# A linear-attention mix on one core: where the output weights are split, a second q buffer, and two tiles' products on VectorE

## The chip, the core and the metric

The kernel runs on one core of a Trainium2 chip. Five engines work side by side, each through its own instructions in program order: TensorE (PE, matrix products into PSUM), VectorE (DVE), ScalarE (ACT), GpSimd (POOL) and SyncE (SP), which here issues every DMA. An instruction that waits holds up all that stand behind it on its engine; engines wait for each other, and for DMAs, by semaphores. The metric is the device time of one execution in microseconds, the median of several runs.

## What is computed

Two branches A and B share the input x (2048 tokens of 448 features) and have their own weights. Each is a linear attention with 16 heads of 28 features and a learned feature map made of two softmaxes; a sigmoid gate mixes them.

```python
qkv = (x @ wqkv).reshape(B, S, 3, H, Dh)            # H = 16, Dh = 28
pq = einsum("bhsd,hdf->bhsf", q, w_phi)              # the same for k
phi_q = concatenate([softmax(pq), softmax(-pq)], -1) # the same for k
kv = einsum("bhsf,bhsd->bhfd", phi_k, v)
z  = einsum("bhsf->bhf", phi_k)
num = einsum("bhqf,bhfd->bhqd", phi_q, kv)
den = einsum("bhqf,bhf->bhq", phi_q, z)[..., None] + 1e-6
branch = (num / den).reshape(B, S, D) @ wo
...
g = sigmoid((x * gate_w).sum(-1, keepdims=True))
out = g * branch_A + (1 - g) * branch_B
```

## The kernel before

The tokens go through in 16 tiles of 128. To keep precision, a matrix is cut into a high part (rounded to the format that TensorE takes) and a low part, the remainder; a product is high x high + low x high + high x low. `split_w` (L99) makes the two parts of a weight: ACT copies the high part, another engine subtracts.

Phase 1 is the loop at L253, one step a tile. PE projects keys (`proj` with `wkh`, `wkl`) and values (`wvh`, `wvl`), 44 matmuls a step, and adds the previous tile to the 56-column sums of keys and values in PSUM (`kv_acc`, L177). DVE makes maxima, minima and shifted values (`shift`), ACT the exponentials, DVE their sums and POOL the quotients (`k_soft`). In steps 2 to 5 the query weights are folded out of `wtb`, a buffer of 4096 columns that holds the raw key and query weights and later, from step 14, the transposed query exponentials of two tiles. In the last three steps the query side of tiles 0 and 1 is begun: `q_front` (L192) subtracts the maximum into `uq`, and SP moves it to DRAM in four pieces and back into `tq` in another order, so that heads stand on partitions. Raw output weights lie in DRAM as `wos`, written there in step 0 in an order of their own.

Between the phases (L303 to L324) come `q_front` of tiles 2 and 3, which write the one buffer `uq` in turn; then the output weights, seven chunks of 128 rows, each loaded from `wos` into one half of `ob` (tile `bd`), split by ACT and POOL into `woh` and `wol` (tiles `wkh` and `wkl`, whose key weights are no longer needed); then the copy of the sums into `kvs` on ACT (L314), their transposition and finish into `kvt` on DVE and POOL; then `gates` of the last three tiles: an exponential on ACT, two DVE instructions, a DMA to DRAM (`gd`), four DMAs back into `gate`, and one POOL instruction (L250).

Phase 2 is the loop at L404. In step i, PE makes the numerators and denominators of tile i (`num`, 256 small matmuls), the query projection of tile i + 4 and the output of tile i - 2 (`out_mm`, 21 matmuls). DVE turns the numerators (`n_turn`) and makes reciprocals; POOL multiplies and adds (`n_rec`, `n_mix`: small products, then L364, the product over 1792 elements, and L367, the sum of the two softmax halves); DVE turns the result back (`o_turn`), ACT makes its high part, DVE and POOL (L386) the low one. Tiles `wvh` and `wvl`, once the value weights, hold the numerators of even and odd tiles in their first 2048 columns and part of the turned result in the next 384.

The order on each engine is that of the code; nothing reorders it.

Of the kernel before, what the change touches and what calls it, by code (L numbers as in the profile page):

```python
# [30 lines left out]
def hedgehog_mix(ctx: ExitStack, tc: tile.TileContext, xd, wv, wkt, wqt, wphi, wo, cmask, cpmask, out):  # L31
# [67 lines left out]
    def split_w(wr, wh, wl, eng):  # L99
        nc.scalar.activation(wh, wr, AF.Copy)  # L100
        eng.tensor_tensor(wl, wr, wh.bitcast(F32), OP.subtract)
# [90 lines left out]
    def q_front(k, ps):  # L192
        seq[k] = len(seq) % 2
        mx = work.tile([P, 2, H], F32, name="qmx")
        p4 = hb(ps[:, :, :D])
        nc.vector.tensor_reduce(mx, p4, AX.X, OP.max)
        for b in range(2):
            nc.vector.tensor_tensor(uq[:, :, b], p4[:, b].rearrange("p (r g) f -> p r g f", r=4),  # L198
                                    mx[:, b].rearrange("p (r g) -> p r g", r=4)[:, :, :, None].to_broadcast([P, 4, 4, DH]),
                                    OP.subtract)  # L200
# [3 lines left out]
        nc.sync.dma_start(tq[seq[k]].rearrange("p c b g f -> p (c b g f)"), m.rearrange("r t c x -> (r t) (c x)"))
# [21 lines left out]
    def q_turn(k):  # L226
        nc.vector.transpose(e_slot(k), eq.rearrange("p s a c f -> p (s a c f)"))  # L227

# [8 lines left out]
    def two_tile():  # L239
        return two.tile([P, 2, 512], F32, name="two")  # L240
# [12 lines left out]
    for t in range(NT):  # L253
# [92 lines left out]

    def n_rec(i):
        rs = work.tile([P, 8, 2, 4], F32, name="crs")
        dd = work.tile([P, 8, 2, 4], F32, name="cdd")
        den = work.tile([P, 4, 2, 4], F32, name="cden")  # L350
        sms[i] = rs, dd, den
        cv = ctrs[i % 2].rearrange("p r b s c m -> p (r b) s c m")
        nc.vector.reciprocal(rs, cv[:, :, :, :, DH + 1])
        nc.gpsimd.tensor_tensor(dd, cv[:, :, :, :, DH], rs, OP.mult)
        nc.gpsimd.tensor_tensor(den.rearrange("p r b c -> p (r b) c"), dd[:, :, 0], dd[:, :, 1], OP.add)

    def n_mix(i):
        rs, dd, den = sms.pop(i)
        nc.vector.reciprocal(den, den)
        nc.gpsimd.tensor_tensor(den, den, gate[:, None, :, :, i].to_broadcast([P, 4, 2, 4]), OP.mult)  # L360
        nc.gpsimd.tensor_tensor(dd, rs, den.rearrange("p r b c -> p (r b) c")[:, :, None, :].to_broadcast([P, 8, 2, 4]),
                                OP.mult)
        c3 = ctrs[i % 2].rearrange("p r b s c m -> p (r b s c) m")[:, :, :DH]
        nc.gpsimd.tensor_tensor(c3, c3, dd.rearrange("p a s c -> p (a s c)")[:, :, None].to_broadcast([P, 64, DH]), OP.mult)  # L364
        o = os_[i] = ph.tile([P, 4, 8, DH], F32, name=f"vs{i % 2}", bufs=1)
        c4 = ctrs[i % 2].rearrange("p r b s c m -> p (r b) s c m")
        nc.gpsimd.tensor_tensor(o.rearrange("p c a f -> p a c f"), c4[:, :, 0, :, :DH], c4[:, :, 1, :, :DH], OP.add)  # L367

# [108 lines left out]
```

## Time and profile before

| what | us |
|---|---|
| median of three runs | 416.49 |
| lowest and highest run | 414.44, 417.14 |
| the profiled execution | 414.41 |
| its span, first to last instruction | 412.6 |

| engine | busy us in the span | share |
|---|---|---|
| PE matmul | 360.6 | 87% |
| DVE | 283.3 | 69% |
| POOL | 233.7 | 57% |
| ACT | 122.9 | 30% |

The page cuts the span into 40 slices of 10.3 us and writes the busy share of each in tenths (9 is 90% or more). PEclk is the clock granted to TensorE, in tenths of full speed.

```profile
PE   7999999999999999999720068999999999997875
```

The digits 2, 0, 0, 6 stand for 206 to 247 us, the passage between the phases. DVE's and POOL's rows have the same hole, and the row of the clock falls to 5 there. In the rows further down, a line of the chain of waits reads: start, duration, engine, tile written, line; a line of the timeline adds the shapes, the count and, in brackets, how long the engine had idled and what released it.

### The profile page before, as it was taken

The page shows a single profiled execution, that of the slowest core. Times are in us where ns is not written, and L with a number is a line of the kernel's source. Part 1 is how long each engine was busy: PE and PEld are TensorE (multiplying, and loading weights), DVE is VectorE, ACT ScalarE, POOL GpSimd, SP SyncE. Part 2 cuts the span into 40 slices and gives each one's busy share as a digit, 9 for nine tenths or more (in the row PEclk, how much of TensorE's full clock was granted, in tenths as well). Part 3 has the DMA queues.
Part 4 walks back from the last instruction along what each step waited for, and adds up shares of the span by engine and source line. Part 5 has one row for each costly group of instructions (what it writes and reads, how often), then busy time and mean ns, then how long its engine had stood idle before and what let it go on. Part 6 is the DMA issues. An engine that isn't in the chain of part 4 may idle for free.

```text
span 412.6 us, 10388 instructions
## 1 busy us (share of the span) xinstructions
PE 360.6 (87%) x4608; PEld 318.8 (77%) x4608; DVE 283.3 (69%) x309; ACT 122.9 (30%) x174; POOL 233.7 (57%) x194
## 2 busy tenths in 40 slices
PE   7999999999999999999720068999999999997875
PEld 7799999999999998998610057888888888875654
DVE  2676667676666666688400079999999999988821
ACT  2634353422222222124011302333323233333112
POOL 0285646164333333143113349999988888889991
PEclk9999999999999999999975558999999999999989
DMA  7937403000000000312432113254433333330101
GB/s 185 286 124 215 175 27 103 2 0 2 2 2 2 2 2 4 89 24 68 119 104 71 41 27 102 82 132 116 113 112 102 100 102 108 113 115 24 48 22 44
DMA packets 24913, 32.09 MB, mean 78 GB/s; under 512 B 3476, under 2 KB 19844, under 8 KB 24836
## 3 DMA queue, kind: packets, MB, share of 16 engines
q1 hardware_dynamic: 24868, 31.43, 26.0%
q8 instruction: 36, 0.59, 0.6%
q14 instruction: 9, 0.07, 0.1%
HBM read 20.40 MB, written 12.62 MB: 80 GB/s over the span
## 4 chain that ended last, share of the span: by engine, by line
PE 65%; DMA 10%; POOL 10%; DVE 7%; SPq 3%; issue 2%; ACT 2%; DVEq 0%; POOLq 0%; ACTq 0%
PE two L134 32%; PE out L393 12%; PE q L134 11%; PE num L339 5%; DMA bd<-wos 5%; PE one L184 3%; DMA qd<-uq 2%; POOL xrb L215 2%; PE two L119 2%; DMA xrb<-in_xt 2%; POOL wvh L364 2%; POOL wvl L364 2%; POOL vs L367 2%; DMA tq<-qd 1%; DVE uq L198 1%
## 5 line engine op out<-in xcount | busy, mean ns | idle before, releaser
L164 POOL TENSOR_TENSOR e<-e,rs 128x896 f32<-128x896 f32 x32 | 53.8, 1703 | 76.7 <-DVE rs L161 70.1
L153 ACT ACTIVATE e<-e 128x896 f32<-128x896 f32 x32 | 30.2, 954 | 112.4 <-DVE e L150 112.3
L393 PE MATMUL out<-wkh,e 128*128 128x448 f32 x224 | 53.7, 376 | 9.6 <-POOL e L386 6.2
L339 PE MATMUL num<-wtb,kvt 32*32 32x128 f32 x2048 | 32.3, 295 | 30.5 <-POOL kvt L318 28.1
L339 PEld LDWEIGHTS num<-wtb,kvt 32*32 32x32 f32 x2048 | 25.6, 107 | 37.6 <-POOL kvt L318 28.4
L393 PEld LDWEIGHTS out<-wkh,e 128*128 128x128 f32 x224 | 41.9, 191 | 16.3 <-POOL e L386 7.7
L134 PE MATMUL two<-wkh,xg 128*128 128x448 f32 x224 | 52.1, 370 | 0.7 <-POOL xg L86 0.4
L134 PE MATMUL two<-wvh,xg 128*128 128x450 f32 (+1 forms) x224 | 50.9, 366 | 0.0
L146 DVE TENSOR_REDUCE mx<-two 128x32 f32<-128x896 f32 x16 | 17.5, 1092 | 42.1 <-PE two L134 42.1
L134 PE MATMUL q<-wqh,xg 128*128 128x448 f32 x168 | 40.9, 384 | 5.6 <-DVE uq L198 5.6
L134 PEld LDWEIGHTS two<-wkh,xg 128*128 128x128 f32 x224 | 40.9, 188 | 5.1 <-POOL xg L86 0.7
L134 PEld LDWEIGHTS two<-wvh,xg 128*128 128x128 f32 x224 | 42.1, 188 | 3.3
L215 POOL TENSOR_TENSOR xrb<-qmn,tq 128x896 f32<-128x896 f32 x16 | 28.1, 1759 | 23.0 <-DVE qmn L214 19.2
L134 PEld LDWEIGHTS q<-wqh,xg 128*128 128x128 f32 x168 | 31.7, 194 | 10.9 <-issue 6.6
L227 DVE STREAM_TRANSPOSE wtb<-xrb 128x2048 f32<-128x2048 f32 x16 | 36.9, 2304 | 3.4 <-ACT xrb L219 3.4
L160 DVE TENSOR_REDUCE sm<-e 128x32 f32<-128x896 f32 x32 | 33.3, 1082 | 1.1
L134 PE MATMUL two<-wvl,xg 128*128 128x450 f32 (+1 forms) x128 | 31.1, 365 | 0.0
L134 PE MATMUL two<-wkl,xg 128*128 128x448 f32 x128 | 30.8, 362 | 0.0
L376 ACT ACTIVATE e<-turn 128x512 fp32r<-128x512 f32 x16 | 9.6, 599 | 69.0 <-DVE turn L373 69.0
L393 PE MATMUL out<-wkl,e 128*128 128x448 f32 x112 | 26.2, 373 | 0.0
L364 POOL TENSOR_TENSOR wvh<-wvh,cdd 128x1792 f32<-128x1792 f32 x8 | 25.8, 3224 | 0.6
L364 POOL TENSOR_TENSOR wvl<-wvl,cdd 128x1792 f32<-128x1792 f32 x8 | 25.8, 3222 | 0.6
(81 smaller groups left out, 617.4 us busy)
## 6 DMA issues: line engine op xcount, KB each, us to landing
qd<-uq SPq DMA_DIRECT2D x64, 112.0 KB, 2.2
tq<-qd SPq DMA_DIRECT2D x16, 448.0 KB, 3.0
out<-bd SPq DMA_DIRECT2D x16, 224.0 KB, 3.4
xrb<-in_xt SPq DMA_DIRECT2D x3, 1024.0 KB
wvr<-in_wv SPq DMA_DIRECT2D x4, 449.0 KB
wtb<-in_wkt SPq DMA_DIRECT2D x8, 224.0 KB, 6.9
wtb<-in_wqt SPq DMA_DIRECT2D x2, 896.0 KB
wos<-in_wo SPq DMA_DIRECT2D x2, 784.0 KB
```

The lines of the kernel that those rows point to most:

```text
L134: nc.tensor.matmul(ps[:, b, :n], x[:, xc, o:o + P], w[:, wc, lo:lo + n], start=i == 0, stop=i == len(terms) - 1)
L146: nc.vector.tensor_reduce(mx[:, 0], p4, AX.X, OP.max)
L153: nc.scalar.activation(e[:, s], e[:, s], AF.Exp)
L160: nc.vector.tensor_reduce(sm[:, s], e[:, s].rearrange("p (h f) -> p h f", f=DH), AX.X, OP.add)
L164: nc.gpsimd.tensor_tensor(e3, e3, rs[:, s, :, None].to_broadcast([P, HA, DH]), OP.mult)
L184: nc.tensor.matmul(kvp[32 * r:32 * r + DH + 1, b, g], v[:, b, h // 2, h % 2], phi[:, :, hs:hs + DH], start=(t == 0 and b == 0 and g == 0), ...
L215: nc.gpsimd.tensor_tensor(eq[:, 1, :, :, :DH], mn.rearrange("p c a -> p a c")[:, :, :, None].to_broadcast([P, 8, 4, DH]), tview(k), OP.sub ...
L227: nc.vector.transpose(e_slot(k), eq.rearrange("p s a c f -> p (s a c f)"))
L339: nc.tensor.matmul(ps[32 * g:32 * g + 32, r, 2 * b + s], kvt[32 * r:32 * r + 32, b, s, g], eTs[i][32 * r:32 * r + 32, s, b, g], start=True ...
L364: nc.gpsimd.tensor_tensor(c3, c3, dd.rearrange("p a s c -> p (a s c)")[:, :, None].to_broadcast([P, 64, DH]), OP.mult)
L376: nc.scalar.activation(hl[:, 0, :MID], ps, AF.Copy)
L393: nc.tensor.matmul(ps[:, :D], a, w, start=n == 0, stop=n == len(terms) - 1)
```

## The change

Four edits.

- A function `split_wo(c)` does one chunk of the output weights: load from `wos` into `wtb`, split on ACT and POOL within `wtb`, and store both parts to DRAM (`wod`). It runs in steps 6 to 12 of phase 1, one chunk a step, the chunks alternating between two places in `wtb`. Between the phases two loads bring the whole of `woh` and `wol` back, 12,544 bytes a partition each.
- `q_front` takes its buffer from a list `uqs`. The list gets a second entry after tile 2: columns 2560 to 3455 of tile `wvh`, so that tiles 3, 5, 7 and so on use that one.
- The tiles `wvh` and `wvl` are taken over for numerators before `q_front(3)` and no longer after the sums.
- In `n_rec` and `n_mix` the last two tiles (14 and 15) use VectorE for the six products and sums that GpSimd does for the others.

```diff
+    wod = [dram.tile([P, 7, D], F32, name=f"wod{i}") for i in range(2)]
...
     def q_front(k, ps):
         seq[k] = len(seq) % 2
+        u = uqs[k % len(uqs)]
...
-            nc.vector.tensor_tensor(uq[:, :, b], p4[:, b].rearrange("p (r g) f -> p r g f", r=4),
+            nc.vector.tensor_tensor(u[:, :, b], p4[:, b].rearrange("p (r g) f -> p r g f", r=4),
...
+    def split_wo(c):
+        n = 3 * D * (c % 2)
+        st = [wtb[:, n + D * i:n + D * i + D] for i in range(3)]
+        nc.sync.dma_start(st[0], wos[:, HP * c:HP * (c + 1), :])
+        split_w(st[0], st[1].bitcast(F32R), st[2].bitcast(F32R), nc.gpsimd)
+        for i in range(2):
+            nc.sync.dma_start(wod[i][:, c], st[1 + i])
...
-            uq = qp.tile([P, 4, 2, 4, DH], F32, name="uq")
+            uqs = [qp.tile([P, 4, 2, 4, DH], F32, name="uq")]
...
         if t > 0:
             kv_acc(t - 1, phi.pop(t - 1))
+        if 6 <= t < 13:
+            split_wo(t - 6)
         if t == NT - 4:
             gates(0, t + 1)
...
-    for k in (2, 3):
-        q_front(k, proj(k, wqh, wql, (D, D), two_tile()))
+    q_front(2, proj(2, wqh, wql, (D, D), two_tile()))
+    cb = [wp_.tile([P, 3592], F32, name=n) for n in ("wvh", "wvl")]
...
+    uqs.append(cb[0][:, 2560:2560 + 2 * D].rearrange("p (r b g f) -> p r b g f", r=4, b=2, g=4))
+    q_front(3, proj(3, wqh, wql, (D, D), two_tile()))
     woh = wp_.tile([P, 7, D], F32R, name="wkh")
     wol = wp_.tile([P, 7, D], F32R, name="wkl")
+    for w, d in ((woh, wod[0]), (wol, wod[1])):
+        nc.sync.dma_start(w.bitcast(F32), d)
     ob = wp_.tile([P, 2, D], F32, name="bd")
     obs = [ob[:, i] for i in range(2)]
-    for c in range(7):
-        nc.sync.dma_start(obs[c % 2], wos[:, HP * c:HP * (c + 1), :])
-        split_w(obs[c % 2], woh[:, c], wol[:, c], nc.gpsimd)
     kv_acc(NT - 1, phi.pop(NT - 1))
...
     def n_rec(i):
+        eng = nc.vector if i >= NT - 2 else nc.gpsimd
...
-        nc.gpsimd.tensor_tensor(dd, cv[:, :, :, :, DH], rs, OP.mult)
+        eng.tensor_tensor(dd, cv[:, :, :, :, DH], rs, OP.mult)
...
-        nc.gpsimd.tensor_tensor(c3, c3, dd.rearrange("p a s c -> p (a s c)")[:, :, None].to_broadcast([P, 64, DH]), OP.mult)
+        eng.tensor_tensor(c3, c3, dd.rearrange("p a s c -> p (a s c)")[:, :, None].to_broadcast([P, 64, DH]), OP.mult)
```

What stands on the engines at the three places that the prediction speaks of. Names with a number are buffers of the pool of that name; a line number is that of the kernel that the list is from. First SP, the queue of DMAs, from the copy-back of query tile 2 to the first stores of phase 2. Before:

```order
L204 DMA tq_293<-qd_81 128x896
L203 DMA qd_82<-uq 32x4x224 x4
L204 DMA tq_294<-qd_82 128x896
L310 DMA bd<-wos 128x1x448 x7
L247 DMA gd<-glog 128x3
L249 DMA gate<-gd 32x4x3 x4
L203 DMA qd_81<-uq 32x4x224 x4
```

The same place after:

```order
L206 DMA tq_295<-qd_83 128x896
L205 DMA qd_84<-wvh 32x4x224 x4
L206 DMA tq_296<-qd_84 128x896
L325 DMA wkh<-wod_80 128x3136
L325 DMA wkl<-wod_81 128x3136
L258 DMA gd<-glog 128x3
L260 DMA gate<-gd 32x4x3 x4
L205 DMA qd_83<-uq 32x4x224 x4
```

Seven chunk loads have become two long ones at the same place, ahead of the last gates' DMAs, and tile 3 is stored from `wvh`.

POOL, from the last step of phase 1 to the first products of phase 2 (`e` are the key exponentials, `wkl` the low output weights, `xrb` the query exponentials). Before:

```order
L164 TENSOR_TENSOR e<-e,rs 128x896 x2
L101 TENSOR_TENSOR wkl<-bd,wkh 128x448 x7
L317 MEMSET kvt 128x16
L318 TENSOR_SCALAR kvt<-kvt 128x2x4
L250 TENSOR_SCALAR gate<-gate 128x4x3
L354 TENSOR_TENSOR cdd<-wvh,crs 128x64
```

After:

```order
L165 TENSOR_TENSOR e<-e,rs 128x896 x2
L333 MEMSET kvt 128x16
L334 TENSOR_SCALAR kvt<-kvt 128x2x4
L261 TENSOR_SCALAR gate<-gate 128x4x3
L368 TENSOR_TENSOR cdd<-wvh,crs 128x64
```

The seven subtractions have left this place (each now stands behind the two `e` products of a step from 6 to 12); the gates' instruction is still ahead of the first products.

DVE in step 15 of phase 2, from the turning of the numerators to the low part of tile 14 (`turn` and `wvh` are the turned result, `cden` and `cdd` the small factors, `vs` the mixed result). Before:

```order
L345 STREAM_TRANSPOSE wvl<-num 128x2048
L353 RECIPROCAL crs<-wvl 128x64
L373 STREAM_TRANSPOSE turn<-vs_4046 128x512
L374 STREAM_TRANSPOSE wvh<-vs_4046 128x384
L359 RECIPROCAL cden<-cden 128x32
L382 TENSOR_TENSOR e<-turn,e 128x512
```

After:

```order
L358 STREAM_TRANSPOSE wvl<-num 128x2048
L367 RECIPROCAL crs<-wvl 128x64
L368 TENSOR_TENSOR cdd<-wvl,crs 128x64
L369 TENSOR_TENSOR cden<-cdd 128x32
L388 STREAM_TRANSPOSE turn<-vs_4064 128x512
L389 STREAM_TRANSPOSE wvh<-vs_4064 128x384
L374 RECIPROCAL cden<-cden 128x32
L375 TENSOR_TENSOR cden<-cden,gate 128x32
L376 TENSOR_TENSOR cdd<-crs,cden 128x64
L379 TENSOR_TENSOR wvl<-wvl,cdd 128x64x28
L382 TENSOR_TENSOR vs_4174<-wvl 128x8x4x28
L397 TENSOR_TENSOR e<-turn,e 128x512
```

Six instructions have come over from POOL, in front of the low part (L382 before, L397 after), which the last third of the output product reads.

More of the change, by code (lines that the diff above doesn't have):

```diff
@@ L202, in q_front @@
         for c in range(4):
-            nc.sync.dma_start(m[:, :, c].rearrange("r t x -> t r x"), uq[32 * c:32 * c + 32].rearrange("p r b g f -> p r (b g f)"))
+            nc.sync.dma_start(m[:, :, c].rearrange("r t x -> t r x"), u[32 * c:32 * c + 32].rearrange("p r b g f -> p r (b g f)"))
         nc.sync.dma_start(tq[seq[k]].rearrange("p c b g f -> p (c b g f)"), m.rearrange("r t c x -> (r t) (c x)"))
@@ L300, in hedgehog_mix @@
             q_front(n, proj(n, wqh, wql, (D, D), two_tile()))
-    for k in (2, 3):
-        q_front(k, proj(k, wqh, wql, (D, D), two_tile()))
+    q_front(2, proj(2, wqh, wql, (D, D), two_tile()))
+    cb = [wp_.tile([P, 3592], F32, name=n) for n in ("wvh", "wvl")]
+    ctrs = [c[:, :2048].rearrange("p (r b s c m) -> p r b s c m", r=4, b=2, s=2, m=HP) for c in cb]
+    oTs = [c[:, 2048:2048 + (7 - MID) * P].rearrange("p (k t) -> p k t", t=P) for c in cb]
+    uqs.append(cb[0][:, 2560:2560 + 2 * D].rearrange("p (r b g f) -> p r b g f", r=4, b=2, g=4))
+    q_front(3, proj(3, wqh, wql, (D, D), two_tile()))
     woh = wp_.tile([P, 7, D], F32R, name="wkh")
     wol = wp_.tile([P, 7, D], F32R, name="wkl")
+    for w, d in ((woh, wod[0]), (wol, wod[1])):
+        nc.sync.dma_start(w.bitcast(F32), d)
     ob = wp_.tile([P, 2, D], F32, name="bd")
     obs = [ob[:, i] for i in range(2)]
-    for c in range(7):
-        nc.sync.dma_start(obs[c % 2], wos[:, HP * c:HP * (c + 1), :])
-        split_w(obs[c % 2], woh[:, c], wol[:, c], nc.gpsimd)
     kv_acc(NT - 1, phi.pop(NT - 1))
@@ L318, in hedgehog_mix @@
     nc.gpsimd.tensor_scalar(kvt[:, :, 0, :, DH], kvt[:, :, 0, :, DH], 1e-6, None, op0=OP.add)
-    cb = [wp_.tile([P, 3592], F32, name=n) for n in ("wvh", "wvl")]
-    ctrs = [c[:, :2048].rearrange("p (r b s c m) -> p r b s c m", r=4, b=2, s=2, m=HP) for c in cb]
-    oTs = [c[:, 2048:2048 + (7 - MID) * P].rearrange("p (k t) -> p k t", t=P) for c in cb]
     gates(NT - 3, NT)
@@ L353, in n_rec @@
         nc.vector.reciprocal(rs, cv[:, :, :, :, DH + 1])
-        nc.gpsimd.tensor_tensor(dd, cv[:, :, :, :, DH], rs, OP.mult)
-        nc.gpsimd.tensor_tensor(den.rearrange("p r b c -> p (r b) c"), dd[:, :, 0], dd[:, :, 1], OP.add)
+        eng.tensor_tensor(dd, cv[:, :, :, :, DH], rs, OP.mult)
+        eng.tensor_tensor(den.rearrange("p r b c -> p (r b) c"), dd[:, :, 0], dd[:, :, 1], OP.add)
     def n_mix(i):
         rs, dd, den = sms.pop(i)
+        eng = nc.vector if i >= NT - 2 else nc.gpsimd
         nc.vector.reciprocal(den, den)
-        nc.gpsimd.tensor_tensor(den, den, gate[:, None, :, :, i].to_broadcast([P, 4, 2, 4]), OP.mult)
-        nc.gpsimd.tensor_tensor(dd, rs, den.rearrange("p r b c -> p (r b) c")[:, :, None, :].to_broadcast([P, 8, 2, 4]),
+        eng.tensor_tensor(den, den, gate[:, None, :, :, i].to_broadcast([P, 4, 2, 4]), OP.mult)
+        eng.tensor_tensor(dd, rs, den.rearrange("p r b c -> p (r b) c")[:, :, None, :].to_broadcast([P, 8, 2, 4]),
                                 OP.mult)
         c3 = ctrs[i % 2].rearrange("p r b s c m -> p (r b s c) m")[:, :, :DH]
-        nc.gpsimd.tensor_tensor(c3, c3, dd.rearrange("p a s c -> p (a s c)")[:, :, None].to_broadcast([P, 64, DH]), OP.mult)
+        eng.tensor_tensor(c3, c3, dd.rearrange("p a s c -> p (a s c)")[:, :, None].to_broadcast([P, 64, DH]), OP.mult)
         o = os_[i] = ph.tile([P, 4, 8, DH], F32, name=f"vs{i % 2}", bufs=1)
         c4 = ctrs[i % 2].rearrange("p r b s c m -> p (r b) s c m")
-        nc.gpsimd.tensor_tensor(o.rearrange("p c a f -> p a c f"), c4[:, :, 0, :, :DH], c4[:, :, 1, :, :DH], OP.add)
+        eng.tensor_tensor(o.rearrange("p c a f -> p a c f"), c4[:, :, 0, :, :DH], c4[:, :, 1, :, :DH], OP.add)
     def o_turn(i):
```

## The prediction, made before the changed kernel was run

> **What bounds the kernel now.** I read the stage table first (busy time of each engine in stretches of the span), then the chain of work that ended last, then the timeline where the chain leaves TensorE. Columns of the stage table: stretch, its length, busy us of PE, PEld, DVE, ACT and POOL with instruction counts, granted TensorE clock, DMA share, GB/s.
>
> ```profile
> 0.00:206.00 206.00, 200.17 (x1971) 181.49 (x1972) 136.20 (x146) 67.14 (x88) 81.62 (x58) 1.00 0.24 71
> 206.00:236.50 30.50, 2.44 (x14) 1.89 (x12) 0.94 (x3) 5.46 (x11) 8.27 (x9) 0.61 0.23 75
> 236.50:255.60 19.10, 14.19 (x406) 11.48 (x406) 15.66 (x18) 3.86 (x5) 12.25 (x14) 0.65 0.21 52
> 255.60:364.40 108.80, 108.73 (x1711) 95.30 (x1711) 102.79 (x112) 35.24 (x51) 95.58 (x82) 1.00 0.39 110
> 364.40:412.60 48.20, 35.07 (x510) 28.68 (x510) 27.73 (x31) 11.19 (x20) 36.03 (x33) 0.96 0.12 44
> ```
>
> PE is full in phase 1 (to 206) and again from 255.6 to 364.4; both stretches are worth nothing to a change that leaves PE's work alone. The 30.5 us from 206.0 are nearly idle on every engine, the next 19.1 are a start-up in which PE is not the bound, and the last 48 are a tail in which POOL is busier than PE. The change works on these three. The chain through the hole:
>
> ```profile
> 207.48 0.34 SPq L204
> ...
> 207.87 5.77 DMA bd<-wos
> ...
> 213.67 0.58 ACT wkh L100
> ...
> 214.32 1.14 POOL wkl L101
> ...
> 229.02 5.08 DMA bd<-wos
> ```
>
> Four such rounds, the last from 229.02, follow one another (load, high part on ACT, low part on POOL, next load into the freed buffer). ACT, in program order, cannot copy `kvs` before the last of them, so `num(0)` starts at 236.5.
>
> **Phase 1, where the splitting goes.** Seven steps (t = 6 to 12) each get one load of 224 KB, one ACT copy, one POOL subtraction, two stores. Rows of step 12 and 13:
>
> ```profile
> 151.87 0.16 ACT L170 ACTIVATE glog<-two 128x1 f32<-128x1 f32 x1
> 153.07 3.36 POOL L164 TENSOR_TENSOR e<-e,rs 128x896 f32<-128x896 f32 x2 [6.65 <-DVE glog L245]
> 159.29 1.89 ACT L153 ACTIVATE e<-e 128x896 f32<-128x896 f32 x2 [7.01 <-DVE e L150]
> ```
>
> ACT is free for 7.0 us before each step's exponentials and POOL for about 6.6 of 10; the added 0.58 on ACT and 1.14 on POOL fit. SP takes its DMAs in order, so load c+1 is issued once POOL has done chunk c and the low store has gone out: 153.07 + 3.36 + 1.14 + about 0.6 = 158.2 in these terms. With a landing of 5.0 to 5.8 (chain rows above) it is there at 163 to 164; ACT reaches its copy at about 162.0 and waits 1 to 2 us of its 7. The step stays PE's: cost 0. If a load took over 7.3 us the loop load + 0.58 + 1.14 + 1.0 would pass the 10.0 us step (that is a rival below). In step 12 the DMAs of the first 13 gates queue on SP behind the last low store, so POOL's gate instruction, which waits for them, comes some 5 us later. That falls into POOL's idle 6.6 and pushes the next L164 by 1 us at most; its reader, the accumulation a step later, has 10: cost 0. The last store has some 50 us before it is read.
>
> **The doubled q buffer.** It removes a wait on DVE (in brackets):
>
> ```profile
> 199.67 0.99 PE L184 MATMUL one<-e,vs 128*29 128x56 f32 x64
> 202.29 0.34 SPq L204 DMA_DIRECT2D tq<-qd  x1
> 202.37 1.16 DVE L198 TENSOR_TENSOR uq<-two,qmx 128x448 f32<-128x448 f32 x2 [1.50 <-DMA qd<-uq]
> 203.67 1.67 PE L134 MATMUL q<-wqh,xg 128*128 128x448 f32 x7 [3.01 <-DVE uq L198]
> ```
>
> L198 ends at about 202.0 instead of 203.53, and PE's first q tile, which waits for it, starts at 202.1. But SP stays in order: the copy-back of tile 2 still waits on tile 2's store (202.29), the stores of tile 3 go out behind that, from 202.7, so what follows on SP is only about 1 us earlier: copy-back of tile 3 at 206.4 (was 207.48). In phase 2 the buffer's earlier reader is a step old and nothing there waited for it: 0.
>
> **The hole and what takes its place.** ACT now copies `kvs` after the accumulation (199.67 + 0.99), DVE turns it after L198 at 202.0, POOL finishes `kvt` at about 203.3, and `num(0)` runs behind the first q tile at 202.1 + 4.75 = 206.9, 29.6 us earlier. It does not follow that the kernel gains 29.6, since phase 2 also needs the last gates. In program order POOL stands at L250 (gates 13 to 15) ahead of every product of tile 0, and SP now has two loads of 1.6 MB ahead of the gates' DMAs. The start-up before:
>
> ```profile
> 236.22 0.35 SPq L247 DMA_DIRECT2D gd<-glog  x1
> 237.72 2.25 SPq L249 DMA_DIRECT2D gate<-gd  x4
> 241.33 0.20 POOL L250 TENSOR_SCALAR gate<-gate 128x12 f32<-128x12 f32 x1 [4.89 <-DMA gate<-gd]
> 242.34 0.35 POOL L354 TENSOR_TENSOR cdd<-wvh,crs 128x64 f32<-128x64 f32 x1 [0.81 <-DVE crs L353]
> 242.76 0.25 POOL L355 TENSOR_TENSOR cden<-cdd 128x32 f32<-128x32 f32 x1
> 243.28 1.75 POOL L215 TENSOR_TENSOR xrb<-qmn,tq 128x896 f32<-128x896 f32 x1 [0.26 <-DVE qmn L214]
> 245.06 0.95 ACT L219 ACTIVATE xrb<-xrb 128x896 f32<-128x896 f32 x1 [8.94 <-POOL xrb L215]
> 245.64 2.98 PE L134 MATMUL q<-wqh,xg 128*128 128x448 f32 x7 [1.10 <-DVE uq L198]
> 246.04 2.31 DVE L227 STREAM_TRANSPOSE wtb<-xrb 128x2048 f32<-128x2048 f32 x1 [0.46 <-ACT xrb L219]
> 255.67 4.75 PE q L134 x22
> ```
>
> Behind POOL stand DVE's reciprocal (L359) and, behind that on DVE, the q work that frees PE's next tile: all wait on G, the time at which L250 runs. When do the gates land? Speed and order of the queue:
>
> ```profile
> 6.40 7.08 DMA xrb<-in_xt
> 7.88 2.69 SPq L97 DMA_DIRECT2D wvr<-in_wv  x4
> 2.00:13.00 11.00, 10.20 (x72) 9.27 (x71) 3.75 (x7) 1.83 (x2) 0.00 (x0) 1.00 1.01 237
> 46.00:48.00 2.00, 2.00 (x14) 1.88 (x11) 1.09 (x1) 0.08 (x1) 2.00 (x2) 1.00 1.04 401
> 213.00:214.00 1.00, 0.00 (x0) 0.00 (x0) 0.00 (x0) 0.33 (x1) 0.00 (x0) 0.50 0.26 100
> ```
>
> The first x piece (256 KB, behind 1.9 MB of key weights) landed at 13.48, when about 237 GB/s x 11 us = 2.6 MB had moved, though 1.8 MB of value weights were queued behind it from 7.88: an early DMA is mostly served first. So I take the gates to come behind both loads. A load with all engines at work moves 401 GB/s (46 to 48) and the old chunk loads 100 on a quarter of them (213 to 214). The new loads have 128 rows of 12.5 KB, contiguous on both sides, so I take 401, and 200 as the far end. Copy-back issued 206.4, its data 207.5 to 209.0 (an estimate: 1.1 from issue to data, 448 KB at 300 to 400); 2 x 128 x 3136 x 4 B = 3.21 MB / 401 = 8.0 us, to 217.0. Of the 1.5 us that `gd` needs alone (236.22 to 237.72) about 1.1 lie ahead of its data, so it lands at about 217.9. From the first gate DMA to POOL 3.6 (237.72 to 241.33): G = 221.5.
>
> Where page and row differ: the Trainium skill, "DMA: Bandwidth & Descriptors", Bandwidth, holds HBM traffic of one core to about 358 GB/s. By it the loads take 9.0 us and every time below would be 1.0 later; the row of 401 in this trace is over that, and I stay with the row.
>
> From G on: 0.20 + 0.35 + 0.25 and the gaps, then L215 1.75, ACT 0.95, so the transposition L227 starts at G + 3.8 (it was G + 4.7, DVE's L353 came last there). From it to PE's first back-to-back q tile 255.67 - 246.04 = 9.6 us of DVE work, unchanged. PE comes to its second q tile after some 12 us of idling; before, its first 7 matmuls took 2.98 (245.64) where 22 take 4.75 at full clock (255.67), that is 1.5 for 7. A tile half of which runs so slowly ends about 0.7 after DVE asks for it at the latest; I take 0.4. So PE is full from 221.5 + 3.8 + 9.6 + 0.4 = 235.3 instead of 255.67: **20.4 us gained**. The output weights are needed only 4.7 us later still, at 240: hidden. From there the 108.8 us of full PE are unchanged.
>
> **The tail.** Tiles 14 and 15 leave POOL for DVE.
>
> ```profile
> 385.64 0.95 POOL e L386
> ...
> 393.83 0.95 POOL e L386
> ...
> 404.57 4.54 PE out L393 x21
> 382.78:389.38 6.60, 4.88 (x143) 3.76 (x141) 4.92 (x7) 1.55 (x3) 5.82 (x8) 1.00 0.06 23
> L364 POOL TENSOR_TENSOR wvl<-wvl,cdd 128x1792 f32<-128x1792 f32 x8 | 25.8, 3222 | 0.6
> L367 POOL TENSOR_TENSOR vs<-wvl 128x896 f32<-128x896 f32 x8 | 16.9, 2110 | 0.6
> L101 DVE TENSOR_TENSOR wvl<-wvr,wvh 128x898 fp32r<-128x898 f32 x3 | 3.1, 1088 | 0.0
> L101 POOL TENSOR_TENSOR wvl<-wvr,wvh 128x898 fp32r<-128x898 f32 x1 | 2.5, 2513 | 3.4 <-ACT wvh L100 3.4
> ```
>
> DVE does 898 elements from SBUF in 1.09, so the product takes about 2.1 (was 3.22) and the sum 1.1 (was 2.11); the four small ones I put at 0.15 each (0.25 to 0.35 on POOL). But DVE already had 4.9 us of work in a tail step (382.78 to 389.38, seven instructions from one turning of numerators to the next). With 3.8 more and the gaps it is 8.9 a step, against POOL's 8.2 before (393.83 - 385.64). So POOL's bound is exchanged for DVE's, and only the overlap of tiles 13 and 14 is gained. From tile 13's sum at 385.64 DVE needs some 5.8 for the turn of tile 13 and the products of tile 14: 391.4; step 15 takes 8.9: 400.3; the last turn and ACT's two copies behind it 2: 402.3. The last 21 matmuls start at 402.6, or at 403.8 if tile 14's run slow at a lower clock (0.96 in the tail as a whole), instead of 404.57: 0.8 to 2.0, I take **1.4**. Bounds: 0 if DVE's products cost as on POOL less the hand-overs, 3 if the small ones are free.
>
> The Trainium skill, "GPSIMD Engine Reference", Specifications, says POOL shares its SBUF interface with DVE and is held up by DVE instructions with two SBUF inputs, which these products are. This trace bears it out weakly (POOL's own 898-wide L101 ran beside DVE's; twice the 448-wide 1.14 of 214.32 would be 2.28, it took 2.51); here it would delay only L386, which ends before DVE's own L382, so the sum stays.
>
> **Sum.** Profiled execution before 414.41 (span 412.6): 414.4 - 20.4 - 1.4 = 392.6. That execution lies 2.1 below the shown median of 416.49 and at the lowest of the three (414.44); I put the median at 394.
>
> **Rivals.**
> 1. The gates' small DMAs are not held by the loads. Then G is SP's time for `gd`, 207.9 (two issues of 0.5 after 206.8), + 5.1 = 213.0, and the time 8.5 lower: 384, median 385. For it: many DMAs can be in flight. Against: the x piece above.
> 2. The loads run at half speed, 200 GB/s (237 in the mixed stretch 2 to 13): 16 us, G = 229.5, time 400.6, median 402.
> 3. The change doesn't do what it says at the hole: the loads run on a quarter of the engines, as the old chunks did at 100 GB/s. Then 32 us, G = 245.6 and PE full at 259.4: 24 later, 416.6, median 418, within 1%. It breaks even at about 115 GB/s. Against: the new source has 128 plain rows.
> 4. Slower: the chunk loads stall phase 1. ACT's copy stands ahead of the next exponentials; with a load of L us each step lasts L + 2.7, so seven steps cost 7 x (L - 7.3); at L = 10.4 the gain of 21.8 is gone, at 11.5 the time is 422. Against: 5.8 is the longest seen.
>
> **Chances.** Forecast (gates behind loads at 300 to 400 GB/s, median 391 to 398): 0.62. Rival 1: 0.15. Rival 2: 0.14. Rival 3: 0.05. Rival 4: 0.04. The range takes in 1 and most of 2: 385 to 402. A measurement here tells about 1%: faster than 412.3 are the forecast, 1 and 2, 0.91; within 1% rival 3, 0.05; slower rival 4, 0.04.
>
> **What would show it.** In the profile after: phase 1 ends at 200 with no new PE gaps, ACT's waits for the chunk loads under 3 us; L198 of tile 3 no longer waits; `num(0)` at about 207; DMA near 400 GB/s from 209 to 217; POOL idle until its gate instruction at 221.5, released by the DMA of `gate`; PE full from 235; the last 21 matmuls some 22 us earlier than at 404.57. POOL's gate instruction at 213 means rival 1, at 229 rival 2. I am wrong at large if PE shows gaps in steps 6 to 13, or if something other than the gates starts phase 2.

## The result, and the profile after

| | median us | runs (lowest to highest) |
|---|---|---|
| before | 416.50 | 4 runs, 414.44 to 417.14 |
| after | 398.44 | 4 runs, 398.22 to 399.1 |

The ratio is 0.9577 (95% interval 0.9542 to 0.9612): faster by 4.2%. The profiled execution after took 398.22, its span is 396.4, which is 16.2 less than before.

The row of PE in the page after, in 40 slices of 9.9 us. The hole is still there; it is two slices shorter, and the 0 in it is now the stretch from about 218 to 228.

```profile
PE   8999999999999999999983089999999999997765
```

The stage table after, cut where the stages end now (columns as in the table of before):

```profile
0.00:206.00 206.00, 202.96 (x1978) 184.85 (x1979) 137.73 (x149) 71.87 (x98) 89.57 (x67) 1.00 0.31 93
206.00:222.00 16.00, 5.59 (x262) 4.30 (x260) 3.82 (x3) 0.95 (x1) 0.00 (x0) 0.69 0.71 265
222.00:240.00 18.00, 10.24 (x159) 8.89 (x160) 13.79 (x16) 3.86 (x5) 14.02 (x14) 0.71 0.27 65
240.00:349.00 109.00, 109.00 (x1713) 95.52 (x1712) 102.91 (x112) 35.45 (x51) 95.76 (x83) 1.00 0.40 110
349.00:396.00 47.00, 32.98 (x502) 26.72 (x500) 35.73 (x43) 10.71 (x19) 21.27 (x19) 0.96 0.11 41
```

In the second row POOL does nothing (before, its row read 1, 3 and 3 tenths in the first three slices of the hole: the seven subtractions) and the DMA engines are busy for 71% of the time: the passage between the phases is now a wait for transfers. SP's queue in the timeline shows which (start, duration of the issue, tile, count):

```profile
199.98 1.75 SPq L205 DMA_DIRECT2D qd<-uq  x4
203.51 0.34 SPq L206 DMA_DIRECT2D tq<-qd  x1
203.94 3.37 SPq L205 DMA_DIRECT2D qd<-wvh  x4
209.40 0.34 SPq L206 DMA_DIRECT2D tq<-qd  x1
209.79 0.42 SPq L325 DMA_DIRECT2D wkh<-wod  x1
210.26 0.42 SPq L325 DMA_DIRECT2D wkl<-wod  x1
210.79 0.36 SPq L258 DMA_DIRECT2D gd<-glog  x1
```

and the chain of work that ended last goes on from there:

```profile
210.79 11.13 DMA gd<-glog
221.94 0.32 SPq L260
...
223.25 1.62 DMA gate<-gd
...
225.04 0.20 POOL gate L261
```

A store of 1.5 KB took 11.13 us to land. PE in the timeline, from the last accumulation of phase 1 to the first full q tile:

```profile
199.90 0.99 PE L185 MATMUL one<-e,vs 128*29 128x56 f32 x64
202.43 1.67 PE L135 MATMUL q<-wqh,xg 128*128 128x448 f32 x7 [1.54 <-DVE wvh L200]
...
207.11 1.90 PE L352 MATMUL num<-wtb,kvt 32*32 32x128 f32 x128
...
228.45 2.98 PE L135 MATMUL q<-wqh,xg 128*128 128x448 f32 x7 [14.45 <-DVE uq L200]
...
238.23 1.67 PE L135 MATMUL q<-wqh,xg 128*128 128x448 f32 x7 [1.30 <-DVE wvh L200]
```

PE is full from 238.23 (255.67 before): 17.4 us gained. Full PE lasts to 347.04, 108.8 as before. From there to the end it is 49.4 us, where it was 48.2: the tail lost 1.2. 17.4 - 1.2 = 16.2, the whole difference of the spans.

### The profile page after: what moved, and what is told of

Its sections match the earlier page's. It is cut to its first block, busy times and chain, and to the rows that moved or that the text cites. A ratio compares the mean times of both kernels' runs of the same rounds, so it can differ in the third digit from the quotient of the medians.

```text
span 396.4 us, 10423 instructions
## 1 busy us (share of the span) xinstructions
PE 360.8 (91%) x4608; PEld 320.3 (81%) x4608; DVE 294.0 (74%) x321; ACT 122.8 (31%) x174; POOL 220.6 (56%) x182
## 4 chain that ended last, share of the span: by engine, by line
PE 71%; DMA 9%; DVE 9%; POOL 4%; SPq 3%; issue 2%; ACT 1%; POOLq 0%; DVEq 0%; ACTq 0%
PE two L135 33%; PE out L408 14%; PE q L135 12%; PE num L352 5%; PE two L120 4%; PE one L185 3%; DMA gd<-glog 3%; DMA qd<-uq 2%; DMA tq<-qd 2%; SPq L205 2%; POOL xrb L217 2%; DVE qmx L198 1%; DVE uq L200 1%; DVE wvh L358 1%; DMA wtb<-in_wkt 1%
## 5 line engine op out<-in xcount | busy, mean ns | idle before, releaser
L408 PE MATMUL out<-wkh,e 128*128 128x448 f32 x224 | 52.8, 373 | 10.9 <-ACT bd L413 6.5
L352 PE MATMUL num<-wtb,kvt 32*32 32x128 f32 x2048 | 31.1, 283 | 2.4 <-DVE wvh L358 2.4
L135 PEld LDWEIGHTS two<-wvl,xg 128*128 128x128 f32 x128 | 24.1, 188 | 2.3 <-POOL wvl L102 0.3
L135 PEld LDWEIGHTS two<-wkl,xg 128*128 128x128 f32 x128 | 24.0, 187 | 1.8 <-DVE wkl L125 0.2
```

Source lines behind the costliest of these rows:

```text
L135: nc.tensor.matmul(ps[:, b, :n], x[:, xc, o:o + P], w[:, wc, lo:lo + n], start=i == 0, stop=i == len(terms) - 1)
L352: nc.tensor.matmul(ps[32 * g:32 * g + 32, r, 2 * b + s], kvt[32 * r:32 * r + 32, b, s, g], eTs[i][32 * r:32 * r + 32, s, b, g], start=True ...
L408: nc.tensor.matmul(ps[:, :D], a, w, start=n == 0, stop=n == len(terms) - 1)
```

## The experiments

The theories that were open with the two profiles side by side. Theory A: the gates' first DMA lands late because of the transfers in flight, and that alone starts phase 2; the second q buffer gains nothing; the products of the last tiles cost time on VectorE. Against it stood that SP's issue, the q tiles or VectorE's own work start phase 2, and that each edit brings its part. Ten kernels were run. Each is the changed kernel with the edit shown.

### The gates' DMAs ahead of the loads

```diff
-    for w, d in ((woh, wod[0]), (wol, wod[1])):
-        nc.sync.dma_start(w.bitcast(F32), d)
...
     gates(NT - 3, NT)
+    for w, d in ((woh, wod[0]), (wol, wod[1])):
+        nc.sync.dma_start(w.bitcast(F32), d)
```

> The changed kernel with the two long loads of the output weights issued behind the last gates' DMAs instead of ahead of them. Theory A: the loads ahead of the gates are what starts phase 2 late. The store of the gates is then issued at about 209.8 and POOL's gate instruction runs at about 214.6 instead of 225.04; TensorE is full from about 13.2 later, 227.8 instead of 238.2, the output weights land at about 226 and are still early enough, and the time falls by about 10, to 388. Theory B: something else holds the gates or the start of phase 2 (a slow small store, VectorE's queue); then POOL's gate instruction stays at 220 or later and the time within 3 of 398.4.

Measured: 390.19 median (388.63 to 390.76, 4 runs), ratio 0.937 (0.9337 to 0.9403), 8.2 us under the changed kernel. SP's queue in its timeline:

```profile
209.36 0.34 SPq L206 DMA_DIRECT2D tq<-qd  x1
209.79 0.38 SPq L258 DMA_DIRECT2D gd<-glog  x1
212.73 2.77 SPq L260 DMA_DIRECT2D gate<-gd  x4
215.54 0.43 SPq L335 DMA_DIRECT2D wkh<-wod  x1
```

`gd` landed after 2.94 instead of 11.13, and POOL's gate instruction ran at 217.05 instead of 225.04. The time followed one for one (8.0 there, 8.2 in the medians). So the gates do start phase 2, and the loads hold them. The 214.6 and the 388 of theory A were missed by 2: from the issue of `gd` to the gate instruction it is 7.3 us here, where they had 4.8.

### Half the dose: one load ahead, one behind

```diff
-    for w, d in ((woh, wod[0]), (wol, wod[1])):
-        nc.sync.dma_start(w.bitcast(F32), d)
+    nc.sync.dma_start(woh.bitcast(F32), wod[0])
...
     gates(NT - 3, NT)
+    nc.sync.dma_start(wol.bitcast(F32), wod[1])
```

> Half of the dose: the load of the high output weights stays ahead of the last gates' DMAs, that of the low ones goes behind them. Theory A (the gates' value gd lands when the loads ahead of it have moved): with 1.6 MB instead of 3.2 ahead, gd lands about 4 us earlier than the changed kernel's 221.94, near 218, GpSimd's gate instruction runs at about 221 (225.0 in the changed kernel, 217.1 with both loads behind), and the time is about 394, half-way between 398.4 and 390.2. The load that is now behind does not slow the four gate DMAs, since SP issues it after they have been issued. Rival (any large load in flight costs the same, whatever its size): gd stays near 222 and the time near 398. Second rival (the loads matter only by SP's issue): gate at 217 to 218, time 390 to 391.

Measured: 394.99 (one run), the gate instruction at 221.00, `gd` landing after 7.74. Between the run before (2.94) and the changed kernel (11.13) that is 59% of the way, the gate instruction stands at 49% of it: about half of the delay for half of the bytes. By this one run it is the amount in flight, not the presence of a load or SP's issue, that sets the wait.

### The gates' DMAs issued by ScalarE

```diff
 def gates(lo, hi):
+        dq = nc.scalar if hi == NT else nc.sync
...
-        nc.sync.dma_start(gd[:, lo:hi], gl)
+        dq.dma_start(gd[:, lo:hi], gl)
...
-            nc.sync.dma_start(gate[32 * r:32 * r + 32, 0, :, lo:hi], gd[:, lo:hi].rearrange("(c t) n -> t c n", c=4))
+            dq.dma_start(gate[32 * r:32 * r + 32, 0, :, lo:hi], gd[:, lo:hi].rearrange("(c t) n -> t c n", c=4))
```

> The changed kernel with the five DMAs of the last gates issued by ScalarE instead of SyncE, so through another queue, the loads where they were. Theory A: the small store waits for the loads because it stands behind them in the same queue. Then from ScalarE it lands in 1.5 to 3 us although the loads are moving at 400 GB/s at that time, POOL's gate instruction runs at about 208 to 213, and the time falls to about 386 to 389. Theory B: it waits because the loads take the DMA engines or the memory whoever issued first; then the store from ScalarE also lands only when the loads are nearly through (after 217), POOL's gate instruction runs at 220 or later, and the time stays within 3 of 398.4.

Measured: 385.31 (one run, span 383.5). ScalarE issued `gd` at 203.90, ahead of both loads (212.86 and 213.33), so the run says nothing on the queue itself: it shows what it is worth not to stand behind SP's stores. Nor are the two queues independent in this program: SP's stores of tile 3 stood 3.6 us for `gd` and 1.3 for a gate DMA, whose semaphores they use again. The gate instruction ran at 211.64 and no longer bound anything, since POOL's next one waited 0.91 for VectorE's reciprocals. PE was full from 226.15, 12.1 earlier than in the changed kernel.

### ScalarE's DMA while the loads move

The loads were put between the stores and the copy-back of tile 2, so that they are moving when ScalarE issues `gd`; the gates' DMAs as in the run before.

```diff
-    def q_front(k, ps):
+    def q_front(k, ps, mid=None):
...
+        if mid:
+            mid()
         nc.sync.dma_start(tq[seq[k]].rearrange("p c b g f -> p (c b g f)"), m.rearrange("r t c x -> (r t) (c x)"))
...
+    def wo_back():
+        for i, d in enumerate(wod):
+            wo2.append(wp_.tile([P, 7, D], F32R, name="wk" + "hl"[i]))
+            nc.sync.dma_start(wo2[i].bitcast(F32), d)
+    wo2 = []
+    q_front(2, proj(2, wqh, wql, (D, D), two_tile()), wo_back)
+    woh, wol = wo2
```

> Both loads go out on SP between the stores and the copy-back of query tile 2 (issued about 201.8 and 202.3, moving about 203 to 211), and the last gates' five DMAs are issued by ScalarE, gd at about 203.9, that is while the loads move. It asks what held gd for 11.1 us in the changed kernel. Theory A1 (a queue is served in its order; another engine's queue isn't behind it): gd from ScalarE lands in 2 to 4 us, by 208, and GpSimd's gate instruction runs at 211 to 212 as when the loads came later (211.6). Theory A2 (every transfer shares the DMA engines with the loads, whichever queue it is in): gd lands only when the loads end, 210 to 212, and the gate instruction runs at 213 to 216. Both: tile 2's copy-back, which is behind the loads on SP's queue, lands near 211 to 213 instead of 207, and the stores of tile 3 likewise, so the time needn't be under the 385.3 of the run with ScalarE's queue alone; 384 to 390.

Measured: 391.14 (one run). SP's queue and ScalarE's in its timeline:

```profile
201.12 0.44 SPq L322 DMA_DIRECT2D wkh<-wod  x1
202.27 0.34 SPq L322 DMA_DIRECT2D wkl<-wod  x1
212.56 0.32 SPq L208 DMA_DIRECT2D tq<-qd  x1
```

```profile
202.60 0.34 ACTq L261 DMA_DIRECT2D gd<-glog  x1
212.56 1.81 ACTq L263 DMA_DIRECT2D gate<-gd  x4
```

Although it was in another engine's queue (the page of this run counts 720 packets in a second hardware queue), `gd` needed 9.96 us and landed when the loads were done. The copy-back of tile 2 on SP shows 212.56 too because it waited 9.7 us for `gd`, whose semaphore it uses again; tile 2's own stores had landed by 202.8. That wait is one reason why the 391.14 lies above the 384 to 390 that were expected, and the gate instruction, at 217.20, above the 213 to 216. Theory A2: the wait is in the DMA engines that both queues feed, not in the order of one queue. The Trainium skill, "DMA: Bandwidth & Descriptors", Issuing engines are not separate DMA queues, says that DMAs of all issuing engines run on the same 16 DMA engines; by that rule the trace agrees. The same page, Queues, rings and completion order, says that a DMA engine takes turns between the queues packet by packet. The trace bears out the turns, but only beside the second load: `gd` is 128 packets of 12 bytes and 16 that signal its landing, nine for each of the 16 DMA engines, and all of them ran between 206.2 and 212.1, in between the second load's packets of 12.5 KB, which take 0.47 us each. Nine such turns are an estimated 4.3 us. Why none ran in the 3.6 us from the issue at 202.60 to 206.2 stays open.

`gd` in seven profiles, with what was moving beside it (in brackets, other profiles with the same order there):

| kernel | moving beside `gd` | us from issue to landing |
|---|---|---|
| before | nothing | 1.50 |
| loads and gates early (below) | the last of a load, 14 GB/s | 1.54 |
| ScalarE's queue | copy-back and stores of q tiles | 4.46 (2.13) |
| gates ahead of the loads | copy-back of a q tile | 2.94 |
| one load ahead | copy-back, 1.6 MB | 7.74 |
| changed kernel | copy-back, 3.2 MB | 11.13 (10.20 to 11.61, four) |
| ScalarE, while loads move | 3.2 MB | 9.96 |

From 2.94 to 11.13 for 3.21 MB is 392 GB/s: the store lands when the loads have moved.

### One q buffer again

```diff
-    uqs.append(cb[0][:, 2560:2560 + 2 * D].rearrange("p (r b g f) -> p r b g f", r=4, b=2, g=4))
```

> The changed kernel with the second q buffer taken away: tile 3 and the later odd tiles use the first buffer again. Theory A: the second buffer gains nothing, since in the changed kernel the second store of tile 3 took SP 1.97 us to issue (204.38) right behind the copy-back of tile 2, and the loads and gates behind it started no earlier; then VectorE's subtraction for tile 3 waits about 1.2 to 1.5 us again, the copy-back of tile 3 is issued within 0.7 us of 209.40, and the time is within 0.7 of 398.4. Theory B (the prediction's step): it brings what follows on SP forward by about 1 us; then the copy-back comes at about 210.4 and the time is 399.4.

Measured: 398.38 median (395.53 to 400.4), ratio 0.9562 (0.9522 to 0.9602), the same as the changed kernel. VectorE waited 2.02 for the first buffer's stores, as before the change, and PE's q tile came 2.0 later (204.42), but the copy-back of tile 3 went out at 209.90, 0.5 later only. From the copy-back of tile 2 to that of tile 3 it is, with one buffer, 5.2 us before the change, 5.4 in the split-alone run below and 6.8 in this run; with two it is 5.9 in the changed kernel and 6.3 to 7.1 in four others. So the stores that start earlier land no earlier, and what is behind them gains nothing. Theory A's reason, the 1.97 that one store took to issue, is not it: in the four others the stores went out in 1.83 to 1.89 together, and the copy-back came no sooner. That they are slowed by tile 2's copy-back, issued just ahead of them, is likely but not shown.

### The tail back on GpSimd

```diff
-        eng = nc.vector if i >= NT - 2 else nc.gpsimd
+        eng = nc.gpsimd
```

> The changed kernel with one part undone: tiles 14 and 15 use GpSimd again for their products and sums. In the changed kernel the stretch from tile 12's numerators turning to the end took 49.4 us (347.04 to 396.4), before the change 48.2 (364.42 to 412.6). Theory A: VectorE loses there, because its long product takes 2.84 instead of the forecast 2.1 and TensorE waits longer for the high part of tile 14; then this kernel's stretch goes back to about 48.2 and the time falls by about 1.2, to 397.2. Theory B (the prediction's step): VectorE gains 1.4 and the 49.4 comes from something else; then the stretch grows to about 50.8 and the time to 399.8.

Measured: 396.93 median (395.82 to 398.64, 6 runs), ratio 0.9544 (0.9512 to 0.9576). That is 1.5 under the changed kernel, but the intervals overlap, so the times alone leave it open. PE's timeline of this run, the last q projection and the last 21 matmuls:

```profile
340.06 0.98 PE L135 MATMUL q<-wql,xg 128*128 128x448 f32 x4
...
387.39 2.98 PE L408 MATMUL out<-wkh,e 128*128 128x448 f32 x7 [0.68 <-ACT bd L413]
```

Between the starts of the two are 47.33 us. The same distance in all profiles: 47.33, 47.33, 47.33, 47.36 and 47.36 in the five with the tail on GpSimd (before among them); 48.49 in the changed kernel and 48.36 to 49.44 in the five others with its tail. VectorE's tail is 1.0 to 2.1 us longer up to there. Part of it comes back behind: in this run the first 7 of the last 21 took 2.98 at a granted clock of 0.50, against 1.69 after, so its span is no shorter (396.8).

### The low part off GpSimd in the tail

What lengthens VectorE's tail? VectorE after, in the timeline, and then GpSimd after at the same moments:

```profile
368.34 0.98 DVE L368 TENSOR_TENSOR cdd<-wvh,crs 128x64 f32<-128x64 f32 x1
...
371.40 2.84 DVE L379 TENSOR_TENSOR wvh<-wvh,cdd 128x1792 f32<-128x1792 f32 x1
...
378.82 0.26 DVE L368 TENSOR_TENSOR cdd<-wvl,crs 128x64 f32<-128x64 f32 x1
...
381.17 2.84 DVE L379 TENSOR_TENSOR wvl<-wvl,cdd 128x1792 f32<-128x1792 f32 x1
```

```profile
368.25 0.99 POOL L401 TENSOR_TENSOR e<-wvh,e 128x384 fp32r<-128x384 f32 x1
371.36 1.01 POOL L401 TENSOR_TENSOR e<-wvl,e 128x384 fp32r<-128x384 f32 x1 [2.12 <-ACT e L392]
381.12 1.00 POOL L401 TENSOR_TENSOR e<-wvh,e 128x384 fp32r<-128x384 f32 x1 [8.76 <-ACT e L392]
```

Each long instruction of VectorE began 0.04 to 0.09 after one of GpSimd; the same L368 without a neighbour took 0.26. The edit takes the neighbour of both products away:

```diff
-        nc.gpsimd.tensor_tensor(hl[:, 1, MID:], oTs[i % 2], hl.bitcast(F32)[:, 0, MID:], OP.subtract)
+        eng = nc.vector if i >= NT - 3 else nc.gpsimd
+        eng.tensor_tensor(hl[:, 1, MID:], oTs[i % 2], hl.bitcast(F32)[:, 0, MID:], OP.subtract)
```

> The one edit: the low part of o_lo1 (L401 of the changed kernel, 1.00 us on GpSimd) for tiles 13 to 15 goes to VectorE, where the products of tiles 14 and 15 already are; GpSimd then does nothing in the last two steps. Theory P (VectorE's product L379 took 2.84 at 371.40 and 381.17 because L401 started on GpSimd at the same moment and the two take turns at SBUF): both products fall to 1.8 to 1.9, L368 of tile 14 (0.98 at 368.34) to about 0.26; VectorE gets about 0.6 more work a step (384 elements); the last 21 matmuls start 1 to 2 us earlier after the full stretch than in the changed kernel (there 388.36 - 347.04 = 41.3), and the median falls from 398.4 to about 397. Theory Q (the product with a broadcast operand simply takes 2.84 on VectorE): both products stay at 2.8, and the median is 398.4 to 399.5.

VectorE in the timeline of this run:

```profile
369.07 0.97 DVE L368 TENSOR_TENSOR cdd<-wvh,crs 128x64 f32<-128x64 f32 x1
...
372.12 2.02 DVE L379 TENSOR_TENSOR wvh<-wvh,cdd 128x1792 f32<-128x1792 f32 x1
374.18 1.09 DVE L382 TENSOR_TENSOR vs<-wvh 128x896 f32<-128x896 f32 x1
375.19 0.55 DVE L402 TENSOR_TENSOR e<-wvl,e 128x384 fp32r<-128x384 f32 x1
```

The product takes 2.02 without GpSimd beside it, so 0.82 of the 2.84 was GpSimd's. (L368 kept its 0.97: a low part of GpSimd still ran there, from 368.97.) The duration is shown; the time is not better: 398.41 median (397.84 to 399.87, 6 runs), ratio 0.9591 (0.9561 to 0.9621), since the 0.55 of the low part now stands in VectorE's row in place of the 0.82. The last 21 matmuls start 48.07 behind the last q projection, 0.4 earlier than in the changed kernel and not the 1 to 2 of theory P; with the tail on GpSimd it is 47.33. So P named the cause of the 2.84 rightly, but not that of most of the tail's loss, which is VectorE's own added work, and its 397 was missed.

The Trainium skill, "SBUF — State Buffer", Who interferes with whom, says that a VectorE instruction with two SBUF inputs and a GpSimd instruction that reads SBUF lock each other out, and that the one issued first goes first. The runs agree: GpSimd was first each time, kept its 1.00, and VectorE stood. No run here has VectorE first.

### The split alone

```diff
-    uqs.append(cb[0][:, 2560:2560 + 2 * D].rearrange("p (r b g f) -> p r b g f", r=4, b=2, g=4))
...
-        eng = nc.vector if i >= NT - 2 else nc.gpsimd
+        eng = nc.gpsimd
```

> Only the first edit is left: the splitting in phase 1, the stores to DRAM and the two long loads; the second q buffer is gone and the products of tiles 14 and 15 are back on GpSimd. Theory A (the split carries the whole gain; the buffer is worth nothing and the tail on VectorE costs about 1.5): 396.5 to 397.5, ratio about 0.953, not slower than the changed kernel's 398.4. Rival (each edit brings its part: buffer about 1, tail about 1): 400 to 401.

Measured: 397.08 median (394.42 to 399.26, 4 runs), ratio 0.9548 (0.9486 to 0.9611). The splitting in phase 1 carries the whole gain; the other edits together add nothing that these runs can tell.

### Two versions beyond

The first is ScalarE's queue with the tail on GpSimd, that is the diffs of two runs above together.

> The run with the last gates' DMAs issued by ScalarE (385.3 in one look), and the products of tiles 14 and 15 back on GpSimd, nothing else. If the tail's 1.5 adds to it: 383.5 to 384.5. GpSimd's gate instruction at 211 to 212 and PE full at about 226 as there; from there 108.8 of full PE and a tail of 48.2 to 48.6, span about 382. Rival: the tail's share is lost in the spread of the runs, 385 to 386.

Measured: 386.45 median (385.19 to 387.89, 4 runs), ratio 0.9296 (0.9236 to 0.9355). That beats the changed kernel by 12.0, but not the single run with VectorE's tail (385.31): the tail's share is lost in the spread, as the rival had it.

The second also puts both loads and the last gates in front of query tile 2:

```diff
+    woh = wp_.tile([P, 7, D], F32R, name="wkh")
+    wol = wp_.tile([P, 7, D], F32R, name="wkl")
+    for w, d in ((woh, wod[0]), (wol, wod[1])):
+        nc.sync.dma_start(w.bitcast(F32), d)
+    gates(NT - 3, NT)
     q_front(2, proj(2, wqh, wql, (D, D), two_tile()))
```

> As the run before, and in front of query tile 2 stand now both loads (SP issues them at about 188 to 190, they move until about 198) and the last gates' instructions (their exponential at about 196.5, gd from ScalarE at about 198.5). Theory A2 (what small DMAs wait for is the loads' traffic in the DMA engines): with the loads over by 199, gd lands within 3 us and the gate instruction runs at 203 to 205; then neither gates nor loads are on the path, the products of tile 0 start when VectorE's reciprocals of num(0) are there (about 212.5), PE is full at 225 to 226, time 382.5 to 384. Rival B (the loads now collide with the stores and copies of query tiles 1 and 2 in the last step of phase 1): tile 2's copy-back lands later than 207, num(0)'s successors start later, time 386 to 390.

Measured: 388.69 median (388.26 to 390.12, 4 runs), ratio 0.9355 (0.9308 to 0.9403); no better than the first. ScalarE and VectorE in its timeline:

```profile
199.01 0.34 ACTq L259 DMA_DIRECT2D gd<-glog  x1
200.55 1.79 ACTq L261 DMA_DIRECT2D gate<-gd  x4
```

```profile
197.77 0.99 DVE L257 TENSOR_SCALAR glog<-glog 128x3 f32<-128x3 f32 x1
198.80 0.18 DVE L258 RECIPROCAL glog<-glog 128x3 f32<-128x3 f32 x1
198.89 1.06 DVE L198 TENSOR_REDUCE qmx<-two 128x32 f32<-128x896 f32 x1
```

A2's part came true (`gd` in 1.54, the gate instruction at 204.49), but its time did not. The gates' two instructions now stand in front of tile 2's maximum on VectorE, and the first of them took 0.99 instead of 0.12 to 0.13: it ended at 198.76, and GpSimd's quotients, which ran beside it, at 198.74. PE's next q tile came 2.57 after the accumulation's end, where it was 1.54, and ran at a low clock (2.95 for seven matmuls, not 1.67). So the time is in B's range, but not by B's mechanism: tile 2's copy-back came 3.61 behind the start of its stores, as in the changed kernel (3.53). The price that the trace shows is in VectorE's order and PE's clock, which neither theory had.

## Why the prediction was right, and where it was not

The forecast was 394.0 in 385 to 402; it came out at 398.44, by the forecast's own mechanism (gates behind the loads at 400 GB/s), with two terms of the sum, the start of full PE and the tail, mis-sized by 5.6 us together (392.6 forecast for the profiled execution, 398.22 measured). The time lies 0.4 above the 391 to 398 that the forecast gave its own case, on the way to rival 2's 402; it is the DMA rows below, not the time, that tell the two apart.

- **Splitting in phase 1, cost 0: right.** The last accumulation starts at 199.90 (199.67 before). ScalarE's copies waited as supposed for the chunk loads, 2.52 at most, inside their idle time:

```profile
104.72 0.58 ACT L101 ACTIVATE wtb<-wtb 128x448 fp32r<-128x448 f32 x1 [2.52 <-DMA wtb<-wos]
...
153.69 0.58 ACT L101 ACTIVATE wtb<-wtb 128x448 fp32r<-128x448 f32 x1 [1.45 <-issue]
```

- **`num(0)` at 206.9: right** (207.11), and right that this is not what phase 2 waits for.
- **The doubled q buffer, "only about 1 us earlier: copy-back of tile 3 at 206.4": wrong.** It went out at 209.40, 1.9 later than before instead of 1.1 earlier. Tile 2's copy-back was itself 1.2 late (203.51 for 202.29): its maximum on VectorE starts 2.19 ahead of the last accumulation, where it started 3.22 ahead before. The delay goes back to tile 0, for whose copy-back VectorE waited 1.41 (to 176.34) where it had waited 0.50 (to 175.20); why that landed later stays open. The stores of tile 3 then took 3.37 to issue, and landed 2.1 after that. The step treated the stores as if nothing but SP's order held them.
- **The loads at 401 GB/s: right.** The changed kernel in stretches:

```profile
212.00:216.00 4.00, 2.00 (x96) 1.54 (x90) 0.91 (x1) 0.00 (x0) 0.00 (x0) 0.52 1.01 421
216.00:219.00 3.00, 0.00 (x0) 0.00 (x0) 0.00 (x0) 0.00 (x0) 0.00 (x0) 0.50 1.03 435
219.00:220.00 1.00, 0.00 (x0) 0.00 (x0) 0.00 (x0) 0.00 (x0) 0.00 (x0) 0.50 0.47 165
220.00:221.00 1.00, 0.00 (x0) 0.00 (x0) 0.00 (x0) 0.00 (x0) 0.00 (x0) 0.50 0.06 25
```

  421 and 435 GB/s in the last column. The limit of about 358 that the prediction cites from the Trainium skill, "DMA: Bandwidth & Descriptors", Bandwidth, does not hold in this trace; the same section gives it for both cores of a memory domain streaming, and this program runs on one. In the last row 0.06 of the engines' time is one DMA engine of 16: 15 of the 16 parts of `gd` had landed by 220.39, the last came at 221.92. In the trace one packet of 16 KB of the queue that the page calls "instruction" took 0.97 us at 215.67, in the middle of the loads. In the split-alone run it came behind `gd`, and `gd` landed after 10.20. That this packet made the one engine late fits, but no run tests it.
- **G = 221.5: 225.04.** Copy-back 3.0 late, `gd` 1.0 longer behind it than forecast (12.54 for 11.5), the gate DMAs 0.5 shorter (3.1). The 11.5 itself has a slip: the loads' end at 217.0 and the 0.4 left of `gd`'s 1.5 make 217.4, not 217.9, so by its own terms the step was 1.5 short, which is what the one late DMA engine cost. From G to full PE 13.2 instead of 13.8: the 0.4 for a slow q tile was not needed. The sum of the four, +2.9, is the difference, rounded, between the 20.4 us forecast and the 17.4 measured; the two that came out shorter than forecast took 1.1 off it, which is luck, and without them it would have been 4.0.
- **The tail, "1.4 gained": 1.2 lost**, outside its own bounds of 0 to 3. The mechanism was right (VectorE becomes the bound of the tail in GpSimd's place), its size and its sign were not. A step was put at 8.9; from the turning of numerators 15 to that of result 15 it is 9.9 (375.89 to 385.77). The product was put at 2.1, which is what it takes alone (2.02); beside GpSimd's low part it took 2.84, twice. The four small ones were put at 0.6 a step and took 0.89, and once 0.98 for the first alone. The prediction took from the Trainium skill, "GPSIMD Engine Reference", Specifications, that GpSimd would be held up; the section says only that the two contend, and the rows show VectorE standing.
- **Rival 1 (the small DMAs are not held by loads) fell** with the 11.13, and more sharply with ScalarE's 9.96. **Rivals 2 and 3 (half or quarter speed) fell** with 421 to 435 GB/s (rival 3's break-even, 3.21 MB in 8.0 + 21.8 us, is 108 GB/s, not 115), **rival 4 (phase 1 stalls)** with the unchanged steps.

The time lies 1.1% above the point forecast, inside its range.

## What to carry to other kernels

When a long chain is taken off the path, look at once for the smallest transfer behind it: here a store of 1.5 KB that the next stage needs landed when the megabytes issued ahead of it had moved, in the one run that tested it from another engine's queue too, so issue it before them (8.2 us here for two moved lines, 12 to 13 from a queue that was free earlier). A buffer that lets stores start sooner was worth nothing here, since they landed no sooner: look at the landing, not at the issue. Before products are moved from GpSimd to VectorE, see which GpSimd instructions will run at the same moment, and add their length to VectorE's.

## What the runs showed of the hardware that was not expected

- Some VectorE instructions are held by a GpSimd instruction that began before them: 2.84 for 2.02, 0.98 for 0.26, 0.99 for 0.13, the last with a single input of 3 columns; GpSimd's had 0.90 to 0.97 still to run. Not all are: the reciprocal L367 of tile 14 kept its 0.55 beside GpSimd's sum (367.75, after).
- Issuing a single DMA can itself hold the queue: the four stores of a q tile take 1.75 us on SP when little moves, but 3.37 in the changed kernel, where one of them took 1.97. The 5.94 and 6.43 in the two runs where ScalarE's gate DMAs went out beside them are something else: there SP's waits for ScalarE's DMAs make up 4.4 and 4.9.
- After PE had idled, its first seven 448-column matmuls took 2.95 to 2.98 instead of 1.6 to 1.7 (14.45 us of idling in the changed kernel, 2.57 in the last run), but 3.01 us of idling at 203.67 before the change cost nothing: a short gap does it in one run and not in another. In the tail the slow stretch falls on the last output tile (387.39, tail on GpSimd) or on the one before it (383.29, after), so a shorter wait there can be given back in part.
